# Loading and casting the first heads of q and k from GpSimd at the start of a fused attention and SwiGLU kernel

## The chip, the core and the metric

The kernel runs on one NeuronCore of a Trainium2 chip. The metric is the device time of one execution in microseconds (us). A core has five engines that run their own instruction streams: TensorE (PE, matrix products; PEld is its weight load), VectorE (DVE), ScalarE (ACT), GpSimd (POOL) and SyncE (SP). SP and POOL issue the DMAs of this kernel, SP to the queue that the profile calls hardware_dynamic, POOL to the one that it calls software_dynamic; only the second one is used here for loads that change the type on the way.

## The reference

There are 8 batches of 8 heads, 576 positions and a head size of 64. Every head computes causal attention whose scores get a bias from running sums, and the result, seen as 4608 rows of 512, goes through a SwiGLU block:

```
scores = q @ k.T / 8
cum    = cumsum(max(s, 0))
scores = where(j > i, -1e9, scores + min(cum[j] - cum[i], 0))
x      = softmax(scores) @ v          # as (4608, 512)
out    = (silu(x @ w_gate) * (x @ w_val)) @ w_out
```

All inputs and the output are float32 in memory. The kernel computes its products in bfloat16 and sums in float32.

## The kernel before

**Tiles and stages.** Heads are worked four at a time; such a half batch is called `hb`, so `hb` 0 holds heads 0 to 3 and `hb` 1 heads 4 to 7. For each half batch there are raw float32 tiles `rawk` and `rawq` (128 partitions, two pairs of heads called `r`, 9 x 64 elements), bfloat16 copies `ck` and `cq`, and a set of `KQ` tiles, named `kq` in the profile, in which k and q stand transposed with the head size along the partitions. The other 64 partitions of a `kq` tile hold the "augmentation" rows: high and low bfloat16 parts of `8 * cumsum` (`HL`) and constants, so that one product gives scores and bias together. A head's scores are made in four pieces (`score_piece`, products of line 373), ScalarE takes their exponential from PSUM (line 383, tile `pt`), and the values product (`av_piece`, line 410, tile `vt` for v) follows; VectorE divides (lines 426 and 427). For the first batch, a product of an identity matrix `ident` with the table `lower` (line 367) adds the causal mask. Rows of x are transposed (line 459) into `XT`, and twelve groups of 128 gate and value columns and the output product follow (lines 643, 664, 666, 677, 700, 749). The order of everything is written out by hand: each engine runs its instructions in the order in which the source issues them, and a bank of PSUM is handed on by `take` and `give`.

**The start.** SP loads `s`, then the four halves of k and q of `hb` 0: `load_one(0, name, (r, r+1))`, line 145, for k and q of pair 0 and then of pair 1. GpSimd makes `ident` and `lower`, clears parts of `kq` (lines 234 and 226, the latter `pads`), and issues the loads of `hb` 1. VectorE prepares constants and runs a chain on `s`: line 240 (relu and scale), 241 (running sum), 244 (high part), 245 (low part), 246 (copy to the other half of `HL`). TensorE runs 32 products of `ident` with itself (`keep_warm`, line 900).

Then comes `hb` 0. ScalarE casts k and q of pair 0 (`cast_half`, line 268), GpSimd those of pair 1 (line 270). TensorE transposes each half in two groups (`row_half`, line 315), and `pe_out` copies a group from PSUM to `kq`: on ScalarE at line 328, on VectorE at line 330. Of pair 0, ScalarE copies both groups of k and the first of q, VectorE the second of q. Head 0 gets its augmentation rows from TensorE rather than from a DMA: `pick` (line 914) multiplies a selection table `sel` by the low and high parts in `HL` for the k side and the q side, and `picked_row` copies the results (ScalarE line 925, VectorE line 929). SP copies the augmentation rows of the other heads (`aug`, line 188).

**What follows it in the queues.** GpSimd issues the five loads of v of batch 0 (line 162; chunks 0 to 4 of 128, the last of 64 positions), casts q of `hb` 1 (line 260), issues the first load of gate weights (line 346), sets constants in `vt` (lines 195 and 196), casts v chunks 0 to 2 (line 173), issues the load of k of `hb` 2, casts chunk 3 and issues more loads. VectorE, after `hb` 0's copies, casts k of `hb` 1 (line 260) and makes ten more copies of line 330; then it casts chunk 4 of v. TensorE's first values products (heads 0 and 1) stand behind the scores of head 5. Within a head the values products go by blocks of 128 rows: block 0 uses chunk 0, block 1 chunks 0 and 1, and so on, so the tenth product of a head is the first that reads chunk 3 and the fifteenth the first that reads chunk 4.

## Time and profile before

| | |
|---|---|
| time, three runs | 373.37, 374.07, 374.59 us; median 374.07 |
| the profiled execution's own time | 373.92 us |
| its span in the profile | 372.0 us |
| busy share | PE 98%, DVE 78%, ACT 65%, POOL 57% |
| DMA | 64.21 MB, mean 173 GB/s |

The span is what the profile shows from the first to the last instruction; 1.9 us of the execution's own time lie around it. The busy shares are averages over very different stretches: in the first 20 us the engines wait for each other, and later TensorE is nearly always the one that is waited for. Lines of the timeline give start, duration, engine, line, operation, output and input tiles and the number of instructions merged in the row, in brackets the idle time before it with what ended it. Lines of the chain give the start, the time and the engine and line of a piece of the work that ended last, followed back from the last instruction.

### The profile page before, as it was taken

To read this page: it belongs to the slowest core of one execution; us is meant where nothing else is said; L and a number is where in the kernel's file an instruction comes from. 1 tells how busy PE (TensorE), PEld (TensorE's weight loads), DVE (VectorE), ACT (ScalarE), POOL (GpSimd) and SP (SyncE) were. 2 spreads that over 40 slices of the span, in tenths; PEclk is the share of its full clock that TensorE was granted. 3 is DMA by queue.
4 is the path that set the end of the run, shared out by engine and by line. 5 is a ranking of instruction groups with operands and counts; after the bars stand their busy time and mean duration, and the time that the engine had idled before them with its cause. 6 is when DMAs were issued, how large, how long until landed. Compare 5 with 4: busy or idle time off the path is not lost.

```text
span 372.0 us, 8786 instructions
## 1 busy us (share of the span) xinstructions
PE 363.2 (98%) x3288; PEld 230.3 (62%) x3288; DVE 291.1 (78%) x585; ACT 239.9 (65%) x470; POOL 212.4 (57%) x325
## 2 busy tenths in 40 slices
PE   7899999999999999999999999999999999999996
PEld 6684556655555557855685558655865585476465
DVE  8978776377985899589967897699868867975984
ACT  8877776778886967688757875786565523323321
POOL 8983556955266547594749464955675516315320
PEclk9999999999999999999999999999999999999999
DMA  7999999799879996996789484994142113002003
GB/s 238 220 254 259 215 272 257 239 299 227 252 172 307 199 268 181 162 285 217 214 179 263 160 185 157 265 210 114 40 121 62 35 30 118 0 3 86 28 0 113
DMA packets 97133, 64.21 MB, mean 173 GB/s; under 512 B 77228, under 2 KB 82724, under 8 KB 97092
## 3 DMA queue, kind: packets, MB, share of 16 engines
q1 hardware_dynamic: 84964, 41.46, 46.9%
q0 software_dynamic: 12128, 22.21, 22.7%
q8 instruction: 25, 0.41, 0.5%
q14 instruction: 16, 0.13, 0.1%
HBM read 37.90 MB, written 19.86 MB: 155 GB/s over the span
## 4 chain that ended last, share of the span: by engine, by line
PE 83%; DVE 10%; DMA 2%; ACT 2%; issue 2%; POOL 1%; DVEq 0%; ACTq 0%
PE banks L643 43%; PE banks L749 17%; PE banks L373 9%; PE banks L410 7%; PE banks L700 5%; DVE kq L330 3%; DMA pk<-ks 2%; DVE pp L666 2%; DVE ht L677 1%; DVE kq L288 1%; ACT th L664 1%; POOL vt L173 1%; ACT pt L383 1%; PE banks L459 1%; PE banks L301 0%
## 5 line engine op out<-in xcount | busy, mean ns | idle before, releaser
L383 ACT ACTIVATE pt<-banks 128x512 bf16<-128x512 f32 (+1 forms) x256 | 120.4, 511 | 29.8 <-PE banks L373 17.1
L643 PE MATMUL banks<-XT,wg 128*128 128x512 bf16 x432 | 111.4, 379 | 0.4 <-DVE pp L666 0.3
L643 PE MATMUL banks<-XT,wv 128*128 128x512 bf16 x432 | 110.9, 379 | 0.1
L664 ACT ACTIVATE th<-banks 128x512 bf16<-128x512 f32 x108 | 64.7, 599 | 56.3 <-PE banks L643 51.4
L666 DVE SCALAR_TENSOR_TENSOR pp<-th,banks 128x512 bf16<-128x512 bf16 x108 | 73.7, 682 | 18.3 <-ACT th L664 18.0
L677 DVE SCALAR_TENSOR_TENSOR ht<-pp,banks 128x512 bf16<-128x512 bf16 x108 | 74.1, 687 | 10.3
L373 PE MATMUL banks<-kq 128*128 128x128 bf16 (+4 forms) x576 | 76.4, 240 | 0.8 <-DVE kq L330 0.3
L686 POOL TENSOR_TENSOR ht<-ht 128x512 bf16<-128x512 bf16 x35 | 40.4, 1154 | 53.3 <-DVE su L684 53.2
L373 PEld LDWEIGHTS <-kq 128*128 128x128 bf16 x576 | 46.1, 98 | 30.7 <-issue 2.4
L643 PEld LDWEIGHTS <-wv 128*128 128x128 bf16 x432 | 38.4, 98 | 36.2 <-issue 0.2
L643 PEld LDWEIGHTS <-wg 128*128 128x128 bf16 x432 | 38.4, 98 | 34.1 <-issue 0.7
L410 PEld LDWEIGHTS <-pt 128*128 128x128 bf16 x960 | 41.8, 98 | 17.7 <-issue 0.7
L388 POOL TENSOR_SCALAR_AFFINE_SELECT pt<-pt 128x512 bf16<-128x512 bf16 x56 | 36.6, 653 | 25.9 <-ACT pt L383 21.7
L410 PE MATMUL banks<-vt,pt 128*128 128x65 bf16 x960 | 46.8, 194 | 0.5 <-DVE ot L427 0.4
L444 POOL DMA_DIRECT2D xs<-ot x24 | 21.7, 904 | 30.4 <-DVE ot L427 28.0
L749 PEld LDWEIGHTS <-ht 128*128 128x128 bf16 x336 | 31.2, 98 | 4.3
L427 DVE TENSOR_TENSOR ot<-banks,rc 128x320 bf16<-128x320 f32 x64 | 31.5, 492 | 2.2
L188 POOL DMA_DIRECT2D kq<-HL x48 | 29.2, 610 | 0.0
L700 PE MATMUL banks<-wo,ht 128*128 128x512 bf16 x96 | 25.8, 379 | 0.0
L749 PEld LDWEIGHTS <-su 128*128 128x128 bf16 x252 | 23.6, 98 | 3.3
L814 POOL TENSOR_TENSOR ysb<-ysb 128x512 f32<-128x512 f32 x12 | 15.2, 1269 | 15.3 <-DVE ysb L808 15.3
L749 PE MATMUL banks<-WS,ht 128*128 128x256 bf16 x168 | 22.9, 273 | 0.0
(101 smaller groups left out, 377.2 us busy)
## 6 DMA issues: line engine op xcount, KB each, us to landing
out_dram<-ysb POOLq DMA_DIRECT2D x32, 256.0 KB, 4.0
rawv<-in_v_dram SPq DMA_DIRECT2D x28, 256.0 KB
rawk<-in_k_dram SPq DMA_DIRECT2D x12, 576.0 KB
rawq<-in_q_dram SPq DMA_DIRECT2D x12, 576.0 KB
xs<-ot POOLq DMA_DIRECT2D x24, 160.0 KB, 3.7
ks<-ck SPq DMA_DIRECT2D x11, 288.0 KB
qs<-cq SPq DMA_DIRECT2D x11, 288.0 KB
rawk<-in_k_dram POOLq DMA_DIRECT2D x3, 576.0 KB, 6.0
```

The lines of the kernel that those rows point to most:

```text
L373: nc.tensor.matmul(sc[:, o : o + w], T[:, 1, e * S + 128 * tj : e * S + 128 * (tj + 1)], T[:, 0, e * S + lo : e * S + hi], start=not maske ...
L383: nc.scalar.activation(pt[:, c0 : c0 + n], sc, AF.Exp, scale=0.125)
L388: nc.gpsimd.affine_select(pt[:, 1088:1600], pt[:, 1088:1600], pattern=[[0, 4], [1, 128]], compare_op=ALU.is_ge, fill=zreg, base=0, channel ...
L410: nc.tensor.matmul(av[:, bi * (D + 1) : (bi + 1) * (D + 1)], pt[:, c0 : c0 + 128], VT[b % 2][:, tj, h, :], start=(tj == 0), stop=(tj == bi),)
L427: nc.vector.tensor_mul(ot[:, :, e * D : (e + 1) * D], av3[:, :, 0:D], rc[:, :, None].to_broadcast([128, NCH, D]),)
L643: nc.tensor.matmul(view(bs, TT), w[:, c, f0 : f0 + 128], xt[:, c, :], start=(c == 0), stop=(c == 3),)
L664: nc.scalar.activation(th, pg, AF.Tanh, scale=0.5)
L666: nc.vector.scalar_tensor_tensor(pp, in0=th, scalar=1.0, in1=pg, op0=ALU.add, op1=ALU.mult)
L677: nc.vector.scalar_tensor_tensor(hp[:, 2 * k2 : 2 * k2 + 2, :].rearrange("p a n -> p (a n)"), in0=pp, scalar=0.5, in1=pv, op0=ALU.mult, op ...
L686: (nc.vector if ft == NFT - 1 else nc.gpsimd).tensor_sub(hp[:, 1:3, :], hp[:, 1:4:2, :], hp[:, 0:3:2, :])
L700: nc.tensor.matmul(view(pys[ts_], DM), hps[ft // 2][:, 2 * (ft % 2) + half, c0 : c0 + 128], WO[j][:, ft % WKO, :], start=(ft == 0), stop=( ...
L749: nc.tensor.matmul(ps, lhs(p), rhs(p), start=(first and p == 0), stop=(last and p == NP - 1), skip_group_check=True,)
```

## The change

The halves of k and q of `hb` 0 are no longer loaded as float32 by SP and cast by ScalarE and GpSimd. GpSimd's first instructions are now loads that write bfloat16 into `ck` and `cq` (`load_first`): k and q of pair 0, then `ident`, then k and q of pair 1, then the loads of `hb` 1. `lower` and the clearing of `kq` come after these, the clearing covers only the padding on the k side, and that of the second set moves behind the constants of `vt`. In `ck` and `cq` of `hb` 0 a pair's elements now stand together, so the transposes read `firsts[name][:, r, j, :]`.

The warming products, 31 now, use a tile `idle` that VectorE sets to zero, in place of `ident`. VectorE's clearing of the augmentation rows moves ahead of the operations that need `ident`. ScalarE makes all four copies of pair 0; VectorE's one is gone. `pick` takes the high parts of both sides first and then the low parts. Of v's five loads, four stand before the cast of q of `hb` 1 and the fifth behind it.

```diff
+    idle = first.tile([128, 128], BF16)
...
+        def load_first(name, r):
+            if r == 0:
+                cts[name, 0] = cp.tile(
+                    [128, J, NR, D], BF16, tag="c" + name, bufs=2, name="c" + name
+                )
+                firsts[name] = cts[name, 0].rearrange("x j r d -> x (j r d)").rearrange(
+                    "x (r j d) -> x r j d", r=NR, j=J
+                )
+            nc.gpsimd.dma_start(
+                firsts[name][:, r].rearrange("x j d -> x (j d)"),
+                SRC[name][0][0, 2 * r : 2 * r + 2, :, :].rearrange(
+                    "e (p j) d -> (e p) (j d)", j=J
+                ),
+            )
...
-        for r in range(NR):
-            load_one(0, "k", (r, r + 1))
-            load_one(0, "q", (r, r + 1))
+        load_first("k", 0)
+        load_first("q", 0)
+        make_identity(nc, ident)
+        load_first("k", 1)
+        load_first("q", 1)
+        for nm in ("k", "q"):
+            load_one(1, nm, eng=nc.gpsimd)
...
+        nc.vector.memset(idle, 0.0)
...
-        make_identity(nc, ident)
+        nc.vector.memset(aug_rows(0, 0)[:, :, S // 2 :], 0.0)
...
-        nc.vector.memset(aug_rows(0, 0)[:, :, S // 2 :], 0.0)
...
-                nc.gpsimd.memset(KQ[i][r][64 * r : 64 * r + 64, :, NR * S :], 0.0)
+                nc.gpsimd.memset(KQ[i][r][64 * r : 64 * r + 64, 1, NR * S :], 0.0)
...
+        pads(0)
         nc.gpsimd.memset(aug_rows(1, 0), 0.0)
-        pads(0)
-        pads(1)
-        for nm in ("k", "q"):
-            load_one(1, nm, eng=nc.gpsimd)
...
-                    ps[64 * r : 64 * r + 64, j - j0, :], ct[:, j, r, :], ident
+                    ps[64 * r : 64 * r + 64, j - j0, :], firsts[name][:, r, j, :], ident
...
-                nc.tensor.matmul(view(b, 128), ident, ident, start=True, stop=True)
+                nc.tensor.matmul(view(b, 128), idle, idle, start=True, stop=True)
...
-        def pick(side):
+        def pick(side, lo):
             b = PICK[side]
-            for lo in range(2):
-                for c0, c1 in ((0, 512), (512, S)):
...
+            for c0, c1 in ((0, 512), (512, S)):
...
-        keep_warm(32, 7)
-        cast_half(0, "k", 0, nc.scalar)
-        cast_half(0, "q", 0, nc.scalar)
+        keep_warm(31, 7)
         aug(0, SP4, range(1, HB))
         aug(1, SP4)
+        load_v(0, range(4), nc.gpsimd)
         row_half("k", 0)
         row_out("k", 0, nc.scalar, nc.scalar)
-        cast_half(0, "k", 1, nc.gpsimd)
-        cast_half(0, "q", 1, nc.gpsimd)
-        load_v(0, range(5), nc.gpsimd)
         row_half("q", 0)
-        pick(1)
-        pick(0)
-        pe_out(0, "q", 0, 0, nc.scalar)
-        pe_out(0, "q", 1, 0, nc.vector)
+        row_out("q", 0, nc.scalar, nc.scalar)
+        for lo in range(2):
+            for kq in (1, 0):
+                pick(kq, lo)
...
         cast_one(1, "q", nc.gpsimd)
+        load_v(0, (4,), nc.gpsimd)
         w_load("g", 0)
         init_vt(0)
+        pads(1)
         for c in range(3):
             cast_v(0, c, nc.gpsimd)
```

More of the change, by code (lines that the diff above doesn't have):

```diff
@@ L148, in load_one @@
                     "(r e) (p j) d -> (e p) r (j d)", e=2, j=J
+                ),
+            )
+        cts = {}
+        firsts = {}
+        def load_first(name, r):
[10 more added lines that the diff above has]
+                    "e (p j) d -> (e p) (j d)", j=J
                 ),
@@ L249 @@
         GP4 = [nc.gpsimd] * 4
-        cts = {}
         def cast_one(hb, name, eng):
@@ L256, in cast_one @@
             src_t = loaded[name, hb]
-            if eng is nc.scalar:
-                nc.scalar.copy(dst, src_t)
-            else:
-                eng.tensor_copy(dst, src_t)
-        def cast_half(hb, name, r, eng):
-            if r == 0:
-                cts[name, hb] = cp.tile([128, J, NR, D], BF16, tag="c" + name, bufs=2, name="c" + name)
-            dst = cts[name, hb][:, :, r, :]
-            src_t = loaded[name, hb][:, r, :, :]
             if eng is nc.scalar:
@@ L312, in pe_transpose_half @@
             ps = tps[name, g][0]
-            ct = cts[name, hb]
             for j in range(j0, j1):
                 nc.tensor.transpose(
-                    ps[64 * r : 64 * r + 64, j - j0, :], ct[:, j, r, :], ident
+                    ps[64 * r : 64 * r + 64, j - j0, :], firsts[name][:, r, j, :], ident
                 )
@@ L908, in row_out @@
                 pe_out(0, nm, g, r, engs[g])
-        def pick(side):
+        def pick(side, lo):
             b = PICK[side]
-            for lo in range(2):
-                for c0, c1 in ((0, 512), (512, S)):
-                    nc.tensor.matmul(
-                        banks[:, b + c0 // 512, 0 : c1 - c0], sel[:, lo, :],
-                        HL[:, lo, 1, c0:c1], start=(lo == 0), stop=(lo == 1),
-                        skip_group_check=True,
-                    )
+            for c0, c1 in ((0, 512), (512, S)):
+                nc.tensor.matmul(
+                    banks[:, b + c0 // 512, 0 : c1 - c0], sel[:, lo, :],
+                    HL[:, lo, 1, c0:c1], start=(lo == 0), stop=(lo == 1),
+                    skip_group_check=True,
+                )
         def picked_row(side):
```

## The prediction

> **What bounds the kernel now.** I read the page first, then the chain of waits for the first 20 us, then GpSimd's, ScalarE's and TensorE's timelines there.
>
> ```profile
> PE 363.2 (98%) x3288; PEld 230.3 (62%) x3288; DVE 291.1 (78%) x585; ACT 239.9 (65%) x470; POOL 212.4 (57%) x325
> ```
>
> TensorE is the bound over the whole span; its other 9 us are where a change of the start can act. The chain there (start, us, engine and line) is VectorE's alone:
>
> ```profile
> 6.97 0.80 DVE HL L246
> 7.77 0.61 DVE kq L330
> ...
> 11.53 1.47 DVE kq L330 x2
> ...
> 15.96 2.83 DVE kq L330 x4
> 18.79 0.04 issue
> 18.83 0.19 PE banks L367
> 19.02 0.03 PE banks L373
> 19.05 0.95 PE banks L410 x28
> ```
>
> The reader is to see that VectorE works without a break until 18.8 us and that TensorE then takes over, at the first values products. From there to 28.3 us every piece of the chain is TensorE's. So what reaches the end is when VectorE gets through its list, unless the values products find something missing. What they read comes from GpSimd:
>
> ```profile
> 4.85 0.91 POOL L145 DMA_DIRECT2D rawk<-in_k_dram  x1
> 5.75 0.74 POOL L145 DMA_DIRECT2D rawq<-in_q_dram  x1
> ...
> 8.25 4.41 POOL L162 DMA_DIRECT2D rawv<-in_v_dram  x5
> 12.65 1.16 POOL L260 CAST cq<-rawq 128x1152 bf16<-128x1152 f32 x1
> ...
> 15.46 1.73 POOL L173 CAST vt<-rawv 128x512 bf16<-128x512 f32 x3
> 17.12 0.71 POOL L145 DMA_DIRECT2D rawk<-in_k_dram  x1
> 17.84 0.62 POOL L173 CAST vt<-rawv 128x512 bf16<-128x512 f32 x1
> ```
>
> Chunk 3 of v is ready at 18.46 us, TensorE begins values at 18.89 and first reads that chunk nine products of 0.034 us (1.02 us for 30) later, at 19.20. GpSimd is busy without a break before it, so this slack of 0.74 us is all there is.
>
> ```profile
> 4.68 0.67 ACT L268 CAST ck<-rawk 128x576 bf16<-128x576 f32 x1 [0.16 <-DMA rawk<-in_k_dram]
> ```
>
> ```profile
> 1.44 3.59 PE L900 MATMUL banks<-ident 128*128 128x128 bf16 x32 [1.44 <-POOL ident masks.py:199]
> 18.83 0.19 PE L367 MATMUL banks<-lower,ident 128*128 128x64 bf16 x1 [0.26 <-DVE kq L330]
> ```
>
> The first half of k lands at 4.68 us on SP's queue (issued at 1.45), its cast ends at 5.35; the warming products end at 5.03; TensorE waits for VectorE just before the values.
>
> **The change on VectorE's list.** It loses one copy of line 330, 7.70 to 8.44 us with its gap: -0.74. It gains the clearing of `idle`; the row of its size (`sel`, line 205) takes 0.17, bounds 0.06 (line 202) and 0.2 with the gap; I take 0.12. Line 929 then also starts as soon as line 246 is done. The moved clearing (0.59) only changes place, and covers the wait for `ident`: VectorE comes to line 215 at 2.27 + 0.12 + 0.62 = 3.0; GpSimd has `ident` 0.57 us (0.81 to 1.38 now) after two half loads, at 2.7. So line 246 ends at 7.9 instead of 7.8, line 929 runs from 7.9 to 8.8 instead of 8.44 to 9.33, and all that follows comes 0.5 to 0.6 us earlier: VectorE ends its copies at 18.25 instead of 18.78. I take 0.54.
>
> **First loads.** One GpSimd half-load issue is not in the trace. Bounds: 0.43 (SP's line 145 for a half) and 0.91 (GpSimd's first whole tile); nearest are GpSimd's 9 KB copies, 0.61 (line 188), and its whole tiles, 0.72; I take 0.66. From issue to landing on that queue: 2.7 is the least for 160 KB (`xs`), 4.5 the first chunk of v (256 KB), 5.3 `rawk` (576 KB, SP's loads still running). For 288 KB that write half of that I take 4.0, ends 2.7 and 5.3. k then lands at 0.81 + 4.0 = 4.8 (3.5 to 6.1) and q about 0.8 later. That is 0.5 before the cast was done. ScalarE, without two casts (1.34) and with one copy more (0.66), would copy from 5.2 to 7.9 and do `picked_row` to 8.7; TensorE picks the low parts when line 245 is done, 7.1 to 7.6. So the first score product comes at about 8.9 instead of 9.38, and VectorE's line 929 is not held up. It would be held up from q landing at 6.2 on; at the late end (k 6.1, q 6.9) the picks end at 8.55 and line 929 starts 0.1 later than now: the gain is gone, no more.
>
> The Trainium skill, page "DMA: Bandwidth & Descriptors", section "Anatomy of one DMA — SWDGE (gpsimd) path", gives 2.0 us plus bytes over 436 GB/s. That would land k at about 3.5 us, an estimate, and nothing of the sum would change, since VectorE's list decides; the rows of this trace for that queue are all longer than the formula.
>
> SP's queue loses four issues (1.85 us), all before its wait for `HL`; the nine copies of line 188 start 0.1 later and are wanted 0.5 earlier. Now head 1's rows, issued at 7.80, are read at 11.04 without a wait. At worst they now cost TensorE 0.6 there; TensorE waited 0.49 for VectorE at 12.41, which covers nearly all of it.
>
> **GpSimd's list.** Start 0.81; four half loads 2.65; `ident` 0.57; two loads of `hb` 1 1.5; `lower` 1.23; `pads(0)` half as wide 0.4; line 234 1.16: v's first load starts at 8.3, as now (8.25). Two casts of line 270 (1.7) paid for what was added. Then four v loads 3.7, cast of q 1.1, fifth v load 0.7, weights 0.76, constants 0.96, `pads(1)` 0.5 (new here), three casts 1.66, load of k 0.72, fourth cast 0.62: chunk 3 at 19.05, against 18.46. With the ends of the half-load issue (0.43 and 0.91) it is 18.1 to 20.05. The fifth v load now starts at 13.1 instead of 11.96; it took 5.7 from issue to landing behind the four others (so at most 18.8; about 17.8 if it lands behind them as now), and VectorE casts it from 18.3 on for 0.55: no wait before the fifteenth product.
>
> **The sum.** TensorE comes to the values at 18.35, does nine products, and waits for chunk 3 from 18.66 to 19.08; now the tenth product is at 19.20. Gain 0.12 of the 0.54. After that the chain is TensorE's, and it carries to the end: later waits on that chain hang on work done in the same order. GpSimd's lag of 0.6 in the loads of k and q of `hb` 2 and of weights is hidden: the gate weights issued at 13.74 landed 7.9 later and are read at 25.06; `ck` of `hb` 2 is cast by 24.4 and read at 26.92. 373.92 - 0.12 = 373.8 for the profiled execution; the median of the runs is 0.15 above it, so 373.9. With chunk 3 at its ends: -0.54 and +0.85, so 373.5 to 374.9.
>
> **Rivals.**
> *GpSimd is late at chunk 3, and it gets slower.* Its program is the only thing that got longer on a full engine. Every tenth past 19.2 is a tenth lost; at the late issue row plus 0.3 for the first issue of all and `pads(1)` beside VectorE's copies, chunk 3 is ready at 20.4: +1.2, 375.3. For it: GpSimd shows no idle time from 0.8 to 22.8. Against: its issues of later whole tiles took 0.71 to 0.76, not 0.91.
>
> *The whole gain, and more.* If half loads issue in 0.45 to 0.55, chunk 3 is no limit and 0.54 stays: 373.5. The stretches to 51 us that end in GpSimd's casts of v (line 173, 2.25 us of the chain from 48.4 on) could also shorten, by up to half of that: 372.4. Against: nothing moves GpSimd's list there ahead, they follow ScalarE.
>
> *The clock.* PE's clock is granted in full in all rows that have a record, but the 32 products take 0.112 each and nine transposes 0.69 in all, so the warming does something. Now it ends at 4.65 and is followed by transposes alone until the picks at 6.3. If it stayed slow for as long again (3.5 us, to 8.7), the 2.4 us of work there (two groups of transposes of 0.5, the picks 0.9, the third group 0.5) would double, and the picks end at 8.65: 0.2 slower than now. If it held to 12, another 2.6 us of work doubles, half of it hidden: +1.5, 375.6. The Trainium skill, "TensorE: Matmul & The Clock Gate", "Part 4: PE-mode transpose", says that transposes don't count as busy, and Part 1 that the window of some 3.4 us runs freely: a rule against this change, which by it could stay slow for one window more; no row here shows the monitor.
>
> *The loads are no earlier.* k landing at 6.1, as worked out: VectorE's gain is gone, chunk 3 no longer counts: 374.2.
>
> **Numbers.** Within 0.3% (1.1 us) is about what a measurement of this kernel can tell from no change. Forecast 0.42; loads no earlier 0.1; GpSimd late 0.2; clock 0.06; whole gain and more 0.22. Past +1.1 go most of the clock and half of the late case, with the spread of the runs (1.2 us): 0.2. Past -1.1 goes the far part of the gain case and some of the spread: 0.25. The rest, 0.55, is same. The range leaves 0.1 on each side: 372.7 to 375.2; the forecast's own is 373.5 to 374.9.
>
> **What would show it.** Right: `ck` transposed at 4.7 to 5.0, first exponential near 9.3, VectorE's copies done near 18.3, TensorE idle 0.3 to 0.5 us among the first values products, released by POOL `vt` L173. Wrong: a wait of TensorE on DMA `ck` or `cq` past 6 us, transposes at the spacing of the warming products, no wait for `vt`, or a wait for it over 0.8 us.

## The result, and the profile after

Over 22 runs each, the changed kernel needs 376.10 us (median; 374.46 to 377.73) and the kernel before 374.48 us (373.37 to 377.44). The ratio is 1.0038, with a 95% interval of 1.0020 to 1.0056: slower by 1.6 us, and outside the forecast's range of 372.7 to 375.2. The profiled execution took 375.91 us, its span is 373.9 us.

The chain of waits of the changed kernel over its first 24 us (start, us, engine and line). Line 266 is the copy in `HL` that was line 246, line 337 VectorE's copies into `kq` (330 before), 380 and 417 the score and values products (373 and 410 before):

```profile
6.59 1.08 DVE HL L265
7.70 1.02 DVE HL L266
8.74 3.37 DMA kq<-HL
...
12.15 0.20 PE banks L380
...
19.44 0.67 DVE vt L192
...
20.16 0.65 PE banks L417 x16
```

Two things are new beside the chain of before. Its two `HL` steps take 1.08 and 1.02 us where they took 0.76 and 0.80. And a DMA stands on the chain: SP's copy of head 1's augmentation rows, issued at 8.74 when `HL` is complete, lands at 12.11. In the kernel before it was issued at 7.80, landed at 10.73 by the trace's semaphore events, and its first reader waited for nothing at 10.78. That reader is not head 1 but head 0's last piece: its block of 128 keys (512 to 640) reaches 64 columns into head 1's part of `kq`. The waits of the changed kernel, first 30 us (total us, times, longest), show the same from TensorE's side, for weight loads and for products:

```profile
PEld L380 <- DMA kq<-HL: 1.5, 2, 1.1
...
PE banks L380 <- DMA kq<-HL: 0.9, 1, 0.9
```

VectorE's timeline of the changed kernel (start, us, line, operation; in brackets the idle time before):

```profile
6.59 1.07 DVE L265 TENSOR_TENSOR HL<-c,HL 64x576 bf16<-64x576 f32 x1
7.70 1.01 DVE L266 COPY HL<-HL 64x1152 bf16<-64x1152 bf16 x1
...
11.83 1.47 DVE L337 COPY kq<-banks 64x640 bf16<-64x640 bf16 x2
13.61 5.81 DVE L337 COPY kq<-banks 64x640 bf16<-64x640 bf16 x8 [0.30 <-PE banks L309]
19.44 0.66 DVE L192 CAST vt<-rawv 64x512 bf16<-64x512 f32 x1
```

and GpSimd's:

```profile
1.33 0.68 POOL L164 DMA_DIRECT2D ck<-in_k_dram  x1 [0.81 <-POOLq L1109]
...
6.28 0.78 POOL L234 TENSOR_SCALAR_AFFINE_SELECT lower<-lower 128x512 bf16<-128x512 bf16 x1
7.00 0.34 POOL L249 MEMSET kq<- 64x64 bf16 x2
7.29 1.11 POOL L258 MEMSET kq<- 64x1216 f32 x1
8.35 3.93 POOL L181 DMA_DIRECT2D rawv<-in_v_dram  x4
...
18.58 0.62 POOL L192 CAST vt<-rawv 128x512 bf16<-128x512 f32 x1
```

The reader is to put the two side by side. Line 265 ends at 7.66, 0.60 us after GpSimd's `affine_select` (7.06); line 266 ends at 8.71, 0.31 us after GpSimd's clearing (8.40). They did not need that time for their own work: below, the same copy takes 0.45 us and the operation before it 0.75 us where GpSimd does nothing. In the kernel before, the copy (line 246) already stood beside a cast of GpSimd and ended at 7.77, 0.31 us after it (7.46):

```profile
6.18 0.75 DVE L245 TENSOR_TENSOR HL<-c,HL 64x576 bf16<-64x576 f32 x1
...
6.54 0.92 POOL L270 CAST ck<-rawk 128x576 bf16<-128x576 f32 x1
```

**Where the time went in these two profiles.** Matching TensorE's weight loads one by one, the changed kernel is 0.84 us earlier at the first transpose, 1.37 later at the rows' first reader, 0.72 to 0.75 later at 20 us, 1.30 later at 56 us and 1.61 later from 133 us to its last product. From 1.37 it falls back to 0.72 because TensorE of the kernel before waits there for VectorE:

```profile
12.41 0.44 PE L301 MATMUL banks<-ident,ck 128*128 128x128 bf16 x5 [0.49 <-DVE kq L330]
```

The first step (0.72) is the subject of the experiments. The second came at a cast of `ck` that GpSimd began at 55.37 us, after 2.5 us of idle time:

```profile
55.37 1.14 POOL L278 CAST ck<-rawk 128x1152 bf16<-128x1152 f32 x1 [2.50 <-PE banks L650]
```

The third came at 131 us, where both executions wait for the transposing DMA `pk<-ks`, 8.61 us long here and 7.22 before. Whether these two belong to the change or to the one execution is taken up again at the last experiments.

### The profile page after: what moved, and what is told of

Read it like the earlier page. It is cut to its first block, busy times and chain, and to the rows that moved or that the text cites. A ratio compares the mean times of both kernels' runs of the same rounds, so it can differ in the third digit from the quotient of the medians.

```text
span 373.9 us, 8740 instructions
## 1 busy us (share of the span) xinstructions
PE 362.5 (97%) x3247; PEld 231.1 (62%) x3287; DVE 292.3 (78%) x585; ACT 240.0 (64%) x469; POOL 213.2 (57%) x327
## 4 chain that ended last, share of the span: by engine, by line
PE 80%; DVE 9%; DMA 4%; issue 2%; POOL 2%; ACT 1%; DVEq 0%; ACTq 0%
PE banks L650 42%; PE banks L756 17%; PE banks L380 9%; PE banks L417 7%; PE banks L707 4%; DVE kq L337 2%; DMA pk<-ks 2%; DVE pp L673 2%; DVE ht L684 1%; DMA out_dram<-ysb 1%; DMA kq<-HL 1%; DVE kq L296 1%; POOL vt L192 1%; PE banks L309 1%; PE banks L466 1%
## 5 line engine op out<-in xcount | busy, mean ns | idle before, releaser
L650 PE MATMUL banks<-XT,wv 128*128 128x512 bf16 x412 | 109.3, 379 | 1.1
L707 PE MATMUL banks<-wo,ht 128*128 128x512 bf16 x90 | 24.8, 379 | 0.3
L400 POOL TENSOR_SCALAR_AFFINE_SELECT pt<-pt 128x64 bf16<-128x64 bf16 x56 | 14.7, 263 | 15.1 <-ACT pt L390 14.9
```

The costliest lines, as they stand in the source:

```text
L650: nc.tensor.matmul(view(bs, TT), w[:, c, f0 : f0 + 128], xt[:, c, :], start=(c == 0), stop=(c == 3),)
L707: nc.tensor.matmul(view(pys[ts_], DM), hps[ft // 2][:, 2 * (ft % 2) + half, c0 : c0 + 128], WO[j][:, ft % WKO, :], start=(ft == 0), stop=( ...
```

## The experiments

Four theories were on record for the first runs. A, the lock: VectorE's `HL` is late because its operations wait for GpSimd's running instruction, and all else follows. B: the smaller edits do it. C: the loads' own traffic slows VectorE. D: the rows' DMA is slow by itself. After the first four runs they became two: the lock, and traffic (head 1's rows wait behind bulk loads). Times stand beside the kernel before on the same chip.

### The two halves of the change

The changed kernel with its copies, picks, pads and v's loads put back as before, so that the loads alone are new:

```diff
-        load_v(0, range(4), nc.gpsimd)
+        load_v(0, range(5), nc.gpsimd)
...
-        row_out("q", 0, nc.scalar, nc.scalar)
-        for lo in range(2):
-            for kq in (1, 0):
+        for kq in (1, 0):
+            for lo in range(2):
                 pick(kq, lo)
+        row_out("q", 0, nc.scalar, nc.vector)
```

> The changed kernel with everything but the loads put back: VectorE makes its copy of the second group of q again, the picks go side by side, the clearing of the padding is whole and in one place, the five loads of v stand together. Theory A (VectorE's chain on s waits for whatever GpSimd has running when it needs their common way to SBUF; in the changed kernel the copy of HL ended 0.31 us after GpSimd's clearing of kq, as it ended 0.31 after a cast before): the clearing now runs some 0.3 us earlier, so the copy of HL ends at about 8.4 to 8.5 us instead of 8.71, VectorE's own copy then costs 0.7, line 935 starts at 9.2 instead of 8.74, and VectorE's copies end at 19.8 to 20.0 instead of 19.41. Whole time 376 to 377. Theory B (the loads are harmless, the loss is in the other edits): the time is that of the kernel before, 374.5, and VectorE's copies end at 18.8.

And the kernel before with everything but the loads (idle warming products, order of the clearings, ScalarE's fourth copy, order of picks, pads and v):

```diff
-        load_v(0, range(5), nc.gpsimd)
+        load_v(0, range(4), nc.gpsimd)
...
-        pe_out(0, "q", 0, 0, nc.scalar)
-        pe_out(0, "q", 1, 0, nc.vector)
+        row_out("q", 0, nc.scalar, nc.scalar)
...
         cast_one(1, "q", nc.gpsimd)
+        load_v(0, (4,), nc.gpsimd)
```

> The kernel before with everything but the loads: SP still loads float32 halves and ScalarE and GpSimd cast them; warming on zeros, ScalarE's fourth copy, the new order of the picks, the smaller padding, v's fifth load behind the cast. Theory A: GpSimd's two casts meet the chain on s as in the kernel before, HL is ready at 7.8 to 8.3 us, one copy less on VectorE, its copies end at 18.2 to 18.7 and the time is 373.9 to 374.5 (same or a little faster). Theory B (the loss is in these edits): HL late or TensorE waiting, VectorE's copies end past 19.3, time near 376.

Measured: the loads alone 375.30 us, ratio 1.0024 (0.9994 to 1.0053); the rest alone 376.06, ratio 1.0036 (1.0008 to 1.0063); before 374.1. From the chain of the loads alone:

```profile
7.69 0.84 DVE HL L267
...
8.56 4.11 DMA kq<-HL
```

and of the rest alone:

```profile
8.03 0.82 DVE HL L247
8.87 3.81 DMA kq<-HL
```

By the times only the second half is shown to be slower; the interval of the first includes no change. In the profiles they have the same signature: `HL` comes after 8.5 instead of at 7.77, the rows are on the chain, and TensorE is 1.17 and 1.04 us behind the kernel before at 20 us. In the rest alone it is VectorE's new order: its chain on `s` begins at 4.39 instead of 3.73, and runs into GpSimd's two casts. So "B, the rest" alone would have been enough to lose the time; the halves do not add up, and both end in the same wait. The profile of the loads alone has something besides: TensorE's granted clock was half of full from 8.10 to 11.51 us, and TensorE itself waited only 0.2 us for the rows. More on the clock below.

### Making HL earlier, twice

The clearing of 1.11 us goes from GpSimd to ScalarE:

```diff
-        nc.gpsimd.memset(aug_rows(1, 0), 0.0)
+        nc.scalar.mul(
+            aug_rows(1, 0).rearrange("p a n -> p (a n)"),
+            one_s[64:128, 0:1].to_broadcast([64, NR * S + 64]), 0.0,
+        )
```

> The changed kernel with one edit: the clearing of 64 x 1216 elements of kq (line 258, 1.11 us) done by ScalarE, which has time there, instead of GpSimd. Theory A: GpSimd goes on from the mask to v's first load at 7.35 us; the low part of HL still waits for the mask and ends at 7.66, the copy of HL then ends at 8.15 if an issue of a DMA doesn't hold VectorE up, at 8.5 if it does, against 8.71; the rows of head 1 land by as much earlier (12.1 to between 11.5 and 11.9) and TensorE's wait for them falls from 0.89 to 0.3 to 0.7. Rival C (the loads' own traffic slows VectorE): the copy of HL still takes 1.0 us and ends at 8.7. Rival D (the rows' DMA is slow by itself): the copy ends earlier, and the rows still land at 12.1.

GpSimd's `lower`, pads and clearing go ahead of the loads of `hb` 1:

```diff
         load_first("q", 1)
-        for nm in ("k", "q"):
-            load_one(1, nm, eng=nc.gpsimd)
...
         nc.gpsimd.memset(aug_rows(1, 0), 0.0)
+        for nm in ("k", "q"):
+            load_one(1, nm, eng=nc.gpsimd)
```

> The changed kernel with GpSimd's list in another order: mask and clearing ahead of the two loads of hb 1, so that they run beside the running sum (line 261), which needs no common way. Theory A: the mask is done at about 6.85 us, the low part of HL ends at 7.2 to 7.5, the copy of HL at 7.6 to 8.0 instead of 8.71; the rows of head 1 land near 11.2 and TensorE waits less than 0.4 for them. The loads of hb 1 are issued 2.5 us later and land at 12 to 13 instead of 10.4, so VectorE's cast of k waits for them until then and its copies end at 19.5 to 20.5. Rival C (the loads' own traffic): the copy of HL still takes 1.0 us.

Measured: 378.90 us, ratio 1.0111 (1.0078 to 1.0143), and 377.51, ratio 1.0090 (1.0055 to 1.0125). Both made it worse. Chain of the first, and its GpSimd:

```profile
7.69 0.77 DVE HL L269
...
8.48 6.23 DMA kq<-HL
```

```profile
7.29 3.54 POOL L181 DMA_DIRECT2D rawv<-in_v_dram  x4
```

Chain of the second:

```profile
8.05 0.58 DVE HL L266
...
8.65 4.90 DMA kq<-HL
```

`HL` did come 0.25 and 0.09 us earlier than in the changed kernel, but the rows then took 6.23 and 4.90 us instead of 3.37. In the first, v's loads start a microsecond earlier (7.29 for 8.35), in the second the two loads of `hb` 1 and the first of v are issued within the 1.9 us before the rows. Theory A, that everything follows from VectorE, fell here: the rows' own time, after their issue, changes more than `HL` does. Part of these two times is the clock: TensorE waited 3.58 and 2.33 us for the rows, and its granted clock was then half of full for 3.4 us, from 15.38 and from 14.08 us on.

In the second run `HL` came much later than expected (7.6 to 8.0). The running sum, line 261, was taken there to be free of GpSimd; it took 1.67 us instead of 1.35, and did so in the two runs with the loads on SP's queue as well. In all three it began at 5.08, beside GpSimd's `affine_select` (4.81 to 5.54).

The lock itself was confirmed. In the first run line 269 ended at 8.46, 0.26 us after the first v issue (8.20): issuing a DMA holds VectorE's copy as a memset does.

### One load more in the kernel before

```diff
             load_one(0, "q", (r, r + 1))
+        load_one(1, "k")
```

> The kernel before plus one load of 576 KB that nobody reads (k of heads 4 to 7 a second time), issued by SP behind its four half loads. VectorE and GpSimd do what they did, HL ends at 7.7 to 7.9. Traffic theory (head 1's rows stand behind the loads that are in flight when they are issued): 576 KB at the 0.4 MB per us that the queues move there are 1.4 us; the rows land at 11.7 to 12.4 instead of 10.7, TensorE waits for them by 0.7 to 1.4 us, and the time is 374.9 to 375.6. Lock theory (what made the kernel slower was only that VectorE's HL came later): HL comes when it did, the rows land at 10.6 to 10.9, 374.0 to 374.3.

Measured: 375.37 us, ratio 1.0003 (0.9972 to 1.0034); the kernel before spread over 373.63 to 377.86 on this chip, so the time decides little. The profile decides. Chain:

```profile
6.97 0.45 DVE HL L247
...
7.45 5.54 DMA kq<-HL
```

and GpSimd:

```profile
7.22 0.73 POOL L271 CAST ck<-rawk 128x576 bf16<-128x576 f32 x1 [0.73 <-DMA rawk<-in_k_dram]
```

The added load held up GpSimd's first cast to 7.22, so VectorE's copy, begun at 6.97, found GpSimd idle and took 0.45 us instead of 0.80: `HL` was ready 0.35 us *earlier* than in the kernel before. The rows, issued at once, landed at 12.99 and TensorE waited 1.94 us for them. That is a wait for the rows without lateness of VectorE. Expected were 11.7 to 12.4; the delay was larger than the 1.4 us of the added bytes. It is one execution: in four of the kernel before and its variants without an added load and with `HL` at 7.77 or 7.78 the rows took 2.85, 2.93, 3.75 and 4.38 us. The 5.54 us here lie outside these, which speaks for traffic and doesn't prove it; the next two runs say more.

### Loads of hb 1 on SP's queue

To empty the queues before the rows are issued, the loads of k and q of `hb` 1 went to SP, right behind the load of `s`; in the second run GpSimd's cast of q also stands ahead of v's loads.

```diff
         for nm in ("k", "q"):
-            load_one(1, nm, eng=nc.gpsimd)
+            load_one(1, nm)
```

> The changed kernel with the loads of k and q of heads 4 to 7 on SP's queue, right behind the load of s, instead of on GpSimd. GpSimd's clearings come 1.5 us earlier, so the op before HL's copy and that copy should be held up less: HL at 8.0 to 8.3 instead of 8.71. But v's first loads are then issued 1.5 us earlier too, from 6.9 us on, two of them ahead of the rows. Lock theory: rows land 3.4 us after HL, at 11.4 to 11.7, 0.5 earlier than in the changed kernel, 375.3 to 375.6. Traffic theory: the rows stand behind two loads of v, as in the run with ScalarE's clearing (6.2 us), and land 4.5 to 6 us after HL, 12.6 to 14.2; 376.5 to 378. A third: SP's two loads beside the first halves make k land after 6 us, and everything starts late: k later than 5.5 and TensorE's first transposes waiting for it.

> As the run before, and GpSimd casts q of heads 4 to 7 ahead of v's five loads, which so come after the rows are issued. Then little is in flight when VectorE is done with HL (8.0 to 8.5). Traffic theory: the rows land 2.0 to 2.8 us after HL, 10.2 to 11.2, TensorE waits for them not at all or by less than 0.3, VectorE's copies end at 18.0 to 18.6, and the time is 373.3 to 374.3, faster than the changed kernel by 1.5 to 2.5 and as fast as the one before or faster. Lock theory: the rows take 3.4 us as before, 11.5 to 11.8, 375.2 to 375.7. Against both: v's third chunk comes 0.5 us later than in the changed kernel, TensorE would wait for it by up to 0.5.

Measured: 378.04 us, ratio 1.0091 (1.0056 to 1.0125), and 378.37, ratio 1.0098 (1.0064 to 1.0132). Both missed; the third possibility named for the first run is what happened. Chain of the first:

```profile
2.01 6.92 DMA cq<-in_q_dram
```

TensorE of the second:

```profile
6.50 1.17 PE L322 MATMUL banks<-ident,ck 128*64 128x128 bf16 x9 [1.89 <-DMA ck<-in_k_dram]
```

The first half of q landed 6.9 us after its issue instead of 3.4 (8.93 for 5.42), with 1152 KB on the other queue beside it. Everything started late, so the two times say nothing about the rows. The clock took part again: the nine transposes took 1.17 us where they took 0.69 in the kernel before, the second profile has no full clock on record before 16.74 us, and in the first it was half of full from 7.96 to 14.79.

The rows' own time does say something. By the traces' semaphore events head 1's rows took 5.03 us in the first run (issued at 8.98, landed at 14.01) and 2.10 in the second (8.53 and 10.63). The two kernels differ only in where GpSimd's cast of q stands: behind four of v's loads in the first, ahead of all five in the second. So v's loads, issued from 6.83 on, are in flight beside the rows in the first; in the second they are issued from 11.98 on, after the rows have landed. From 10 to 11 us the DMA engines moved 253 GB/s in the first and 30 in the second. Expected for the rows under traffic were 2.0 to 2.8 us, under the lock 3.4. It is one execution of each, but 2.10 us is the shortest time of these rows in any profile here, 1.27 less than the shortest of the changed kernel. That is the best evidence for traffic.

The second run also gives a clean reading of the lock: GpSimd waited for the load of q from 6.9 to 10.9, and VectorE's copy of line 266 took its bare time, with loads in flight (theory C falls with it):

```profile
8.05 0.45 DVE L266 COPY HL<-HL 64x1152 bf16<-64x1152 bf16 x1
```

### The first step of the forecast alone

ScalarE makes the fourth copy in the kernel before, nothing else:

```diff
-        pe_out(0, "q", 1, 0, nc.vector)
+        pe_out(0, "q", 1, 0, nc.scalar)
```

> The kernel before with one thing of the change alone: ScalarE makes the fourth copy of k and q of pair 0, VectorE's copy after HL is gone. Nothing that GpSimd or the queues do is touched, so HL should end where it did (7.7 to 7.8 us). List theory (VectorE's list alone sets the start): its copies end 0.5 to 0.7 us earlier, near 18.2, and the time falls by that, to 373.4 to 373.6. Rows theory (head 1's rows set it as soon as VectorE has room): the rows land where they did (10.6 to 10.8), TensorE waits for them for the first time by 0.2 to 0.5 us, and of the 0.67 at most 0.3 is left: 373.8 to 374.1.

Measured: 376.67 us, ratio 1.0018 (0.9978 to 1.0058); the profiled execution 374.27, span 372.3 against 372.0 before. `HL` was as before and nobody waited for the rows. VectorE's list did come earlier at first, by 0.52 us: line 929 began at 7.92 instead of 8.44, and the copies of `hb` 1 at 11.01 instead of 11.53. Then it was lost. VectorE and TensorE:

```profile
11.01 2.94 DVE L330 COPY kq<-banks 64x640 bf16<-64x640 bf16 x4
14.78 1.45 DVE L330 COPY kq<-banks 64x640 bf16<-64x640 bf16 x2 [0.82 <-PE banks L301]
```

```profile
14.22 0.68 PE L301 MATMUL banks<-ident,cq 128*128 128x128 bf16 x9 [0.64 <-POOL cq L260]
```

GpSimd's five issues of v took 4.76 us here (4.41 before), so its cast of q of `hb` 1 ended at 14.18 and VectorE then idled 0.82 us. A run with that cast ahead of v's fifth load takes this limit away:

```diff
-        load_v(0, range(5), nc.gpsimd)
+        load_v(0, range(4), nc.gpsimd)
...
         cast_one(1, "q", nc.gpsimd)
+        load_v(0, (4,), nc.gpsimd)
```

> The kernel before with the two parts of the change that load no queue earlier and hold up nobody: ScalarE's fourth copy, and the cast of q of heads 4 to 7 ahead of v's fifth load. HL as before (7.7 to 7.8). In the run with the fourth copy alone VectorE waited 0.82 us for TensorE, which waited for that cast until 14.18. List theory with that corrected: the cast ends 0.7 earlier, 13.2 to 13.5, VectorE does not wait, its copies end at 18.1 to 18.4, the values begin 0.4 to 0.6 us earlier than before (18.89) and the time is 0.4 to 0.6 us under that of before on the same chip. If head 1's rows take it: they land at 10.6 to 10.8, TensorE waits for them by up to 0.3, a gain of 0.2. If v's last load comes too late: VectorE's cast of it starts after 18.9, no gain.

Measured: 374.69 us, ratio 1.0000 (0.9966 to 1.0034). No gain again. Line 929 began at 8.52, after 0.74 us of waiting for the picks: the first two groups of transposes took 1.17 us each, with a full clock on record only from 7.46 us on. And this time the rows were late, by their own time (4.38 us) and with `HL` at 7.78; its waits:

```profile
PE banks L373 <- DMA kq<-HL: 1.0, 1, 1.0
```

### The changed kernel again, and with work put before the rows

> The changed kernel as it is, again, beside the two others and on their chip. If the two causes found are those of every execution, HL ends at 8.5 to 8.8 (0.3 us after GpSimd's clearing), head 1's rows land at 11.8 to 12.7, TensorE waits for them by 0.6 to 1.4 us, and the time is 1.0 to 2.5 us over that of the kernel before. If the wait was an accident of one profile, the rows land before 11.4 here and the time is within 1 us of before.

```diff
-        scores(1)
         half_batch("k")
+        scores(1)
```

> The changed kernel with the transposes of k of heads 4 to 7 ahead of head 1's scores in TensorE's order, so that there is work while head 1's rows are on their way. The rows land when they did (11.8 to 12.7) and HL ends when it did. Rows theory in its narrow form (their wait costs VectorE the 0.30 us it idled at 13.3): VectorE's copies run on, its last one ends 0.3 us earlier, near 19.1, and 0.2 to 0.5 us of the 1.9 come back: 375.4 to 375.7. If the whole loss hangs on the wait of TensorE (0.89 and 0.43): 374.3 to 374.9. If the lateness of VectorE's HL alone counts: no change, 375.9.

Measured, before at 375.11 us: the changed kernel 376.13, ratio 1.0036 (0.9999 to 1.0074); with the transposes of k first 376.16, ratio 1.0034 (1.0005 to 1.0064). The chain of the changed kernel in this execution:

```profile
8.72 5.18 DMA kq<-HL
```

and with k first:

```profile
8.72 4.88 DMA kq<-HL
...
13.65 0.20 PE banks L380
13.86 0.50 PE banks L309 x9
```

The same program, `HL` ready at the same 8.71, and the rows took 5.18 us instead of 3.37. This execution took 378.63 us; it is 3.17 us behind the kernel before at the rows' first reader, 3.72 from 20 to 130 us, and 3.15 at 134 us, behind the wait at 131 us that the kernel before has and this execution has not. So the wait is no accident of one profile, but its size is one of each execution.

Not all of the 3.72 us is the wait. In the first profile 0.63 us of 1.37 was made up again between the first reader and 20 us; here 0.55 is added. The busy times of this execution in two stretches (us; busy time and instructions of PE, PEld, DVE, ACT and POOL; then the granted share of the TensorE clock, the DMA engines' busy share and GB/s), and a row of TensorE:

```profile
11.00:14.40 3.40, 0.69 (x9) 0.40 (x8) 2.23 (x3) 0.98 (x3) 3.35 (x5) 1.00 0.98 247
14.50:17.90 3.40, 3.40 (x28) 2.59 (x26) 1.45 (x2) 2.23 (x6) 3.18 (x9) 0.50 1.02 174
```

```profile
15.32 1.15 PE L309 MATMUL banks<-ident,ck 128*128 128x128 bf16 x9
```

TensorE did almost nothing while it waited, 0.69 us of 3.40, and then ran at half its clock from 14.51 to 17.93 us: nine transposes took 1.15 us that took 0.67 in the first profile, where the clock was full. The third profile of the changed kernel, below, shows the same from 14.58 to 17.99. What that costs can be estimated from the other traces. From the rows' first reader to 20 us the lag fell by 0.63 to 1.00 us in the five executions that waited for the rows at full clock, and it rose by 0.25 to 0.82 in the four whose clock was halved behind the wait (this one, the third, and the two runs with `HL` earlier); so a halving costs some 0.9 to 1.8 us there. That the wait brings it on is likely but not tested: four executions with a wait of 2.3 us or more had it within 1 us of the wait's end, one with 2.41 us (the next run) had not, and those with waits of 0.9 to 1.9 us had not.

The second run could not tell what it was meant to. Its chain shows why: TensorE waits for the rows in head 0's last piece (line 380 at 13.65), and the moved transposes (line 309) stand behind that. The expectation had the wrong first reader.

### Work put before the first reader

So head 0's last piece now goes behind k's transposes too, and q's go ahead of head 2's scores; once in the changed kernel and once in the kernel before, with the changed kernel a third time beside them:

```diff
         score_piece(0, 2)
-        score_piece(0, 3)
...
-        scores(1)
         half_batch("k")
+        score_piece(0, 3)
+        scores(1)
+        half_batch("q")
         score_piece(2, 0)
         score_piece(2, 1)
-        half_batch("q")
```

> The changed kernel with the first reader of head 1's rows moved: it is head 0's last piece, whose block of 128 keys reaches 64 columns into head 1. That piece now stands behind the transposes of k of heads 4 to 7, and those of q stand ahead of head 2's scores. HL ends at 8.7 as before, the rows land where they land (12.1 to 13.9). Rows theory: TensorE makes the transposes of k at 11.9, VectorE's copies run on without the gap of 0.30, and a late landing costs TensorE less by the 0.5 us of those transposes and more where VectorE stays busy: 0.3 to 1.0 us under the changed kernel, 375.1 to 375.8 against 376.1. Rival (VectorE's own lateness is the whole of it): no change.

> The same reordering in the kernel before. Where its rows land at 10.7 nothing is gained at 20 us (VectorE's copies are without a gap already); where they land at 12 to 13, as in two of its variants, 0.3 to 1.0 us. Rows theory: the median falls by 0.1 to 0.5 us and the highest times fall more than the lowest. Rival: the transposes of q ahead of head 2's scores wait for GpSimd's cast until 13.8 and hold up the scores, 0.2 to 0.6 us slower.

> The changed kernel once more, to be compared with the run where the first reader stands later on the same chip. The rows land 3 to 5.5 us after their issue, at 11.8 to 14, and the time is 1.0 to 2.5 us over that of the kernel before.

Measured, before at 374.70 us: the changed kernel so reordered 375.76, ratio 1.0017 (0.9985 to 1.0048); the kernel before so reordered 375.69, ratio 1.0006 (0.9976 to 1.0035); the changed kernel 376.18, ratio 1.0022 (0.9988 to 1.0056). VectorE of the changed kernel, third time:

```profile
15.34 1.44 DVE L337 COPY kq<-banks 64x640 bf16<-64x640 bf16 x2 [1.91 <-PE banks L309]
17.65 3.67 DVE L337 COPY kq<-banks 64x640 bf16<-64x640 bf16 x5 [0.87 <-PE banks L309]
```

and of the reordered one:

```profile
11.82 7.22 DVE L337 COPY kq<-banks 64x640 bf16<-64x640 bf16 x10
```

The rows landed at 13.56 and 13.18, 4.8 and 4.5 us after their issue. In the first VectorE idled 2.8 us, behind TensorE that waited 2.36 us for the rows and then ran at half clock from 14.58 to 17.99, and TensorE was 3.08 us behind the kernel before at 26 us. In the second TensorE waited 0.67 us, its clock stayed full, VectorE ran on and TensorE was 1.03 behind. By the estimate above some 1 of these 2 us is the clock; the rest is the wait for the rows, taken off the path by other work in most of its length. Then ScalarE is next: its exponentials stand in the chain for 4.26 us there. Of the 2 us the medians show 0.4, which is within their uncertainty. In the kernel before the same order costs 0.55 us at 19 us, as its rival said, and nothing is won: nobody waits for the rows in its profile. No kernel run here beats the one before.

### Taking the rows out of the way

Heads 1 to 3 of the first batch take their rows from a part of `kq` that ScalarE has cleared by 4.5 us, so that they are issued long before they are read. These three kernels leave out the bias of these heads:

```diff
-                    HL[bh : bh + 1, :, :, :],
+                    HL[bh : bh + 1, :, :, :] if hb else KQ[1][1][32:36, :, 0:S],
```

> The kernel before, but the rows of heads 1 to 3 are copied from a part of kq that ScalarE has cleared by 4.5 us instead of from HL (it leaves out the bias of these heads in the first batch). They are issued near 4.6 us and can't be late. Rows theory (run to run the time varies because these rows land at a different time): the highest runs go, the spread of some 4 to 6 us shrinks to 2 or less, the median falls to 373.0 to 374.2. Rival (the spread is the clock's or the rest of the kernel's): the spread and the median stay those of before on this chip.

> The changed kernel with the same substitution. HL still ends near 8.7. Rows theory (most of the loss is that head 1's rows, issued 0.94 later, are now the last thing to come): no wait for the rows, VectorE's copies run on and end near 19.1, and the kernel is within 0.0 to 1.0 us of the kernel before with the same substitution. What is then left is VectorE's 0.3 and what the later loads do at 55 us. Lock theory (the lateness of VectorE itself, not of the rows): the difference stays at 1.3 to 2.0 us. Expected 374.0 to 375.0 against 376.1.

> The kernel before with ScalarE's fourth copy and v's fifth load behind the cast of q of heads 4 to 7, and the same substitution. With the rows out of the way this measures the first step of the forecast by itself, that VectorE's list of copies sets the start. If it does: the copies end at 18.1 to 18.4, the values begin 0.4 to 0.6 earlier and the time is 0.4 to 0.6 us under that of the kernel before with the substitution. If something else stands there (the picks, ScalarE's longer list): the first score at 9.5 or later and VectorE waiting for the picks, a gain under 0.2 or none.

Measured, before at 374.59 us (373.37 to 377.52): the kernel before with early rows 374.33 (373.38 to 376.88), ratio 0.9989 (0.9959 to 1.0018); the changed one 375.22 (374.08 to 376.43), ratio 1.0006 (0.9979 to 1.0034); the third 374.17 (373.29 to 378.48), ratio 0.9997 (0.9962 to 1.0033). VectorE in the first:

```profile
11.54 7.25 DVE L330 COPY kq<-banks 64x640 bf16<-64x640 bf16 x10
```

in the second:

```profile
11.82 7.24 DVE L337 COPY kq<-banks 64x640 bf16<-64x640 bf16 x10
```

in the third, TensorE first:

```profile
9.69 0.38 PE L367 MATMUL banks<-lower,ident 128*128 128x512 bf16 x1 [0.91 <-ACT kq L925]
```

```profile
8.20 0.89 DVE L929 TENSOR_SCALAR kq<-banks,r_q,r_k 64x576 bf16<-64x576 f32 x1 [0.42 <-PE banks L914]
...
10.50 1.01 DVE L260 CAST ck<-rawk 128x1152 bf16<-128x1152 f32 x1
11.54 7.26 DVE L330 COPY kq<-banks 64x640 bf16<-64x640 bf16 x10
```

Three readings.

First, the rows. Without their wait the changed kernel's copies run on without a gap and end at 19.06, 0.27 us after those of the first run (18.79). With the wait TensorE was 0.74 behind the kernel before at 20 us in the first profile, and 3.72 and 3.07 in the two others. So VectorE's lateness is worth 0.27 there. The rest is mostly the rows: 0.5 in one execution; in the two others it is 3.45 and 2.80, of which some 0.9 to 1.5 (the estimate above) is the halved clock and 1.5 to 2.3 the wait for the rows itself. By medians the two kernels with early rows are 0.89 us apart where they were 1.6, but each median is uncertain by half a microsecond or more, so the split in the final time is not better known than that.

Second, the spread. We expected it to shrink to 2 us in the first run. It went from 4.2 to 3.5, so most of the kernel's spread has other causes. The granted clock is one that is on record: the highest of these runs, 376.88 us, is the only one whose mean granted clock was under 0.998 (0.991).

Third, the forecast's first step. In the third run VectorE has one copy less, nobody waits for rows or for GpSimd's cast of q, and its ten copies begin at 11.54 as in the first. Three things stand behind that. Line 929 waits 0.42 us for the picks and begins at 8.20; in this execution the first half of q came late (ScalarE waited 0.50 us for it) and the first nine transposes took 1.17 us, with a full clock on record from 6.44 on. ScalarE, with one copy more, ends `picked_row` (line 925) at 9.64, and TensorE waits 0.91 us for that. And VectorE's cast of `ck`, begun at 10.50, takes 1.01 us instead of 0.76 beside GpSimd and ends at 11.51, as ever. So the copy that was taken from VectorE was worth nothing in the end in any of the three runs without it, each time for another reason. The run with the fourth copy alone is the one where the picks were in time, and there VectorE's list was 0.52 us ahead at 11 us. No execution here has both, the picks and the cast of q in time, so whether the 0.5 us can be kept is not shown.

The two later steps of the first comparison also look different now. Of the runs with the changed kernel's start, neither the second and third profile of it nor the one with early rows has the wait of 0.55 us at 55 us. And the wait for `pk<-ks` at 131 us is on the chain in the kernel before (7.22) and in the changed kernel with early rows:

```profile
118.27 8.25 DMA pk<-ks
```

but not in the kernel before with early rows, which is 0.53 us ahead of the plain one from there on, and not in the second profile of the changed kernel. Both are waits that one execution has and another has not.

## Why the prediction was wrong

**The first loads: right.** k landed at 4.52 us (4.8 forecast, 3.5 to 6.1) and q at 5.42; the half-load issues took 0.68, 0.56, 0.56 and 0.54 (0.66 taken). That all rows of that queue are longer than the formula holds for their medians, not for every transfer: the shortest took 1.87 us for 9 KB and 2.35 for 256 KB.

**VectorE's list: wrong, and the first failed step.** "So line 246 ends at 7.9 instead of 7.8": it ended at 8.71. The forecast moved VectorE's operations as if their durations were their own. They are not: 0.45 us for the copy alone, 0.80 beside GpSimd's cast before, 1.01 beside the clearing after; for the subtraction 0.75 alone and before, 1.07 after. The row of before, 0.80, already held 0.35 us of waiting. Of the 0.94 us that `HL` came later, 0.17 is the later start of the chain on `s` (3.90 for 3.73), 0.22 its first operation (0.78 for 0.56), 0.32 the subtraction and 0.21 the copy. The diff moved `lower`'s `affine_select` and a clearing of 1.11 us to stand beside these operations; GpSimd's list was timed in the forecast for what it delivers, never for what it holds up.

The Trainium skill, "SBUF — State Buffer", section "SBUF: two separate sides", states the rule: VectorE in its two-port fast modes and GpSimd share a pair of ports that one of them holds for a whole instruction while the other is blocked. Here VectorE's blocked copies ended 0.25 to 0.31 us after GpSimd's instruction (memset, cast and DMA issue alike), which agrees; the page would have told to look at GpSimd's timeline beside line 246.

**"At worst they now cost TensorE 0.6 there ... covers nearly all of it": wrong, and the step that decides.** The rows were taken to need the 2.9 us that they had in one profile. They were issued 0.94 later instead of 0.1, took 3.37 us, and TensorE waited 0.89 for them, 0.43 more at a weight load of head 2's scores. The cover that the forecast counted on was there: of the 1.37 us lost at the first reader 0.65 was made up at 12.41. It was the loss that was over twice the 0.6 taken. In two other executions of the same program the rows took 5.18 and 4.83 us, in its variants 2.10 to 6.23, in those of the kernel before without an added load 2.85 to 4.38. The reader was misplaced as well: head 0's last piece reads them at 10.78, 0.26 us before the place that the forecast looked at. That the rows stand behind other loads is the likely reason: in the run with one load more `HL` was earlier and the rows landed 2.26 us later, and with v's loads put behind them they took 2.10 us instead of 5.03. These are single executions, and the rows' time varies by 1.8 us in one program. The bound from both sides should have come from the rows of this trace for 9 KB on the other queue, 4.2 us, which the prediction did not use. What exactly a row waits for in the 16 DMA engines is open.

The Trainium skill, "DMA: Bandwidth & Descriptors", section "Queues, rings and completion order", says that each DMA engine takes turns between queues, a packet of some 9 to 17 descriptors at a time, so that a small DMA would wait for some packets of the others and not for all their bytes. The runs neither show nor exclude that; the 2.10 to 6.23 us from issue to landing is what such turns have to explain.

**The gain that should have been there: wrong.** The 0.54 us were VectorE's 0.74 less what came back. In the kernel before with the copy moved, 0.52 us of it showed at 11 us in one run and was gone at 14 us, behind GpSimd's cast of q; in the two runs with that cast moved ahead, the picks, and in one of them a cast of VectorE beside GpSimd, took it before 12 us. What is late next behind VectorE was asked for GpSimd's v alone.

**GpSimd's list: right.** Chunk 3 was ready at 19.20 us (19.05 forecast, 18.1 to 20.05), before the values products began at 19.52. The rival of a late chunk 3 did not come about. Chunk 4, which was to cause no wait before the fifteenth product, cost 0.1 us: VectorE came to it late and cast it from 19.44 to 20.10.

**The clock: beside the path at the start, and on it later.** Two groups of nine transposes took 1.17 us each where they took 0.69 before; that is the slowness which the rival named, but for these two groups only. VectorE was later than TensorE there, so it cost nothing. It isn't the change's either: a full clock is on record from 7.13 us on in this profile and from 4.27 and 4.34 in the two others of the same program, where the transposes took 0.69; in the kernel before and its variants it begins between 4.25 and 7.46. What no rival named is the halving behind a long wait for the rows, some 0.9 to 1.5 us in two of three profiles. For the runs without a profile only the mean granted clock is on record; 3.4 us at half clock would make it 0.995 over 374 us. Of 45 runs of the changed kernel 18 had 0.995 or less, with a median of 377.2 us, against 375.6 for the rest; of 125 runs of the kernel before, 22, with 377.1 against 374.6. So the changed kernel is 1.0 us slower among the rest, and has such a clock over twice as often. The runs come from several chips, where in them the slower clock falls is not on record, and no run tested the clock by itself.

**The sum.** Forecast -0.12 at 20 us; measured +0.72 to +0.75 in the first profile: +0.27 from VectorE and the rest from the rows. The remaining +0.9 of that profile came at 55 and 131 us, from waits that other executions of the same kernel lack; those had more of the rows and the halved clock instead. The range left out the case that did come: no rival was a transfer that VectorE's lateness puts on the path, although the rows landed 0.05 us before their first reader in the kernel before.

## What to carry to other kernels

Read the duration of a VectorE operation together with what GpSimd was doing: a bare time has to be looked for, and when GpSimd's list is reordered, check which of its instructions now stands beside each operation on VectorE's path. A small DMA issued in the middle of bulk loads has no fixed latency; if something reads it at once, take its slack and not its duration, and look for the widest row of such DMAs in the trace. When a wait of TensorE grows to some microseconds, look at the granted clock behind it before all that follows is put down to the wait. Moving work from the engine on the path to another pays only as far as what is late next, and here that left nothing.

## What the runs showed of the hardware that was not expected

A DMA issue of GpSimd holds VectorE's copy just as a memset does: 8.46 against the issue's end at 8.20, and 0.57 us instead of 0.45 in the run with the clearings first. A 9 KB copy on SP's queue took 3.37, 5.18 and 4.83 us in three executions of one program, and 5.54 in the kernel before with 576 KB more in flight. It took 5.03 us behind v's loads and 2.10 ahead of them. The first half of q, 144 KB written, landed after 3.4 us in the changed kernel and after 6.9 us with 1152 KB more on the other queue. After waits for the rows of 2.33 to 3.58 us TensorE's granted clock was half of full for 3.4 us in four executions; after one of 2.41 us it was not.
